# Positions in orbits of twelve: a folded transform in place of full DFT matrices, and cast loads issued by GpSimd

## The chip, the cores and the metric

The kernel runs on one core of a Trainium2 chip. The metric is the device time of one execution in microseconds. Before the change its median over three runs is 419.32 us (418.64 to 421.66). Engines are named as in the profile: PE (TensorE), DVE (VectorE), ACT (ScalarE), POOL (GpSimd), SP (SyncE).

## The reference

A linear attention with cosine and sine weights feeds a gated long convolution. The sizes are batch B = 8, heads H = 8, S = 576 positions, head dimension 64, model width 512.

```python
theta = pi/2 * arange(S) / S
phi(x) = concat([max(x, 0) * cos(theta), max(x, 0) * sin(theta)], -1)    # 64 -> 128 features
kv  = einsum('bhsf,bhsd->bhfd', phi(k), v);  z = sum(phi(k), axis=2)
x   = einsum('bhsf,bhfd->bhsd', phi(q), kv) / (einsum('bhsf,bhf->bhs', phi(q), z)[..., None] + 1e-06)
x   = x.transpose(0, 2, 1, 3).reshape(B, S, 512)
x1, x2, x3 = split(x @ w_proj, 3, axis=-1)                               # 512 columns each
conv = irfft(rfft(x2, axis=1) * rfft(filter_fft, axis=0), n=S, axis=1)   # along the positions
out  = (x1 * conv * x3) @ w_out
```

## The kernel before

All matrix work is in f16 with f32 sums. A batch's 576 positions lie in five tiles of 128 (the last holds 64; buffers are padded to 640). A framework schedules the instructions of each engine, starting from the order of the emit calls, and puts the semaphores in; pools of a fixed number of buffers say when a tile may be written again.

Batches run through a software pipeline. In cycle `cyc`, the input DMAs of batch cyc+1 are issued, the second half of the attention of batch cyc-1 is done (`emit_attn_B`), then the projections and the forward DFT of batch cyc-2 (`emit_moe_part1`), the first half of the attention of batch cyc interleaved with the transposes of batch cyc-1 (`emit_sec3`), the inverse DFT and output of batch cyc-2 (`emit_moe_part2`), and phi of batch cyc+1. In words, per batch:

- **Loads** (L203): 15 transfers by SP, one per tile of q, k and v, in f32; each position row of a head is a run of 256 B. Weights come in f32 by SP and are cast by ACT (L125) and DVE (L129, L132).
- **phi**: 20 ACT instructions (L220, L224), relu with a scale per partition, f32 to f16. DVE casts v (L228); POOL writes the column of ones (L229).
- **Attention**: PE forms kv (L264), 40 matmuls of 65 columns; transposes phi(q) (L273), 40 times 128 columns; forms the numerators (L322), 40 of 65. DVE takes reciprocals (L332, L333) and scales (L342), five instructions per head. PE transposes back per pair of heads (L291), 20 of 128; DVE (L278, L296) and ACT (L280, L298) copy transposes out of PSUM.
- **Projections**: x1 and x3 (L363, L368), 64 matmuls of 288 columns; the gate x1*x3 (L375, L376); x2 (L383), 20 of 512, evicted by ACT (L388).
- **Forward DFT** (L398, L404): 289 frequencies in tiles of 128, 128 and 33 against five position tiles, cosine and sine: 30 matmuls of 512. DVE multiplies with the filter's transform in six instructions per frequency tile (L422 to L427).
- **Inverse DFT** (L442 to L454): per channel tile of 128, cosine and sine over three frequency tiles, for 289 and for 287 positions: 48 matmuls. DVE multiplies with the gate out of PSUM (L459, L462).
- **Output** (L471), 20 of 512, ACT evicts (L476), SP stores five times (L477).

PSUM is split in three pools: 2 banks for kv, 3 for transposes, 3 for everything else. DFT tables are computed on the chip (`emit_dft_gen`, DVE and ACT); the filter is transformed in cycle 1.

## Time and profile before

| | before |
|---|---|
| median of three runs | 419.32 us |
| span of the profiled execution | 417.9 us |
| that execution's time outside the span, by the median | 1.4 us |
| PE matmul busy | 341.8 us, 82% |
| DVE busy | 237.3 us, 57% |
| ACT busy | 240.5 us, 58% |
| POOL busy | 6.6 us, 2% |
| DMA | 43.58 MB, mean 104 GB/s |

The profile is one execution. "Busy" on PE counts overlapping matmuls once, with modelled ends, so the spacing of two matmul starts says more about their cost than the duration printed. The granted TensorE clock is below full in many slices, and has to be taken with every PE figure. A batch appears in the chain of waits as a stretch of x2, DFT, inverse and output matmuls, with ACT, DVE and DMA pieces between output and the next x2.

### The profile page before, as it was taken

The page shows a single profiled execution, that of the slowest core. Times are in us where ns is not written, and L with a number is a line of the kernel's source. Part 1 is how long each engine was busy: PE and PEld are TensorE (multiplying, and loading weights), DVE is VectorE, ACT ScalarE, POOL GpSimd, SP SyncE. Part 2 cuts the span into 40 slices and gives each one's busy share as a digit, 9 for nine tenths or more (in the row PEclk, how much of TensorE's full clock was granted, in tenths as well). Part 3 has the DMA queues.
Part 4 walks back from the last instruction along what each step waited for, and adds up shares of the span by engine and source line. Part 5 has one row for each costly group of instructions (what it writes and reads, how often), then busy time and mean ns, then how long its engine had stood idle before and what let it go on. Part 6 is the DMA issues. An engine that isn't in the chain of part 4 may idle for free.

```text
span 417.9 us, 7205 instructions
## 1 busy us (share of the span) xinstructions
PE 341.8 (82%) x2606; PEld 199.5 (48%) x2606; DVE 237.3 (57%) x884; ACT 240.5 (58%) x429; POOL 6.6 (2%) x53
## 2 busy tenths in 40 slices
PE   0252937899959997699959995899979988999994
PEld 0141326546546455455546554545654546455441
DVE  5787326638394475548385739547563756372370
ACT  4993697677964677556684568358435222514502
POOL 1000000000000000000000001000000000000000
PEclk9995777699996999599999999699989997999998
DMA  9957999942677935441664064001300030003003
GB/s 183 227 208 260 227 206 170 193 91 51 164 177 119 173 89 172 107 89 25 190 143 99 0 165 127 2 13 38 115 2 0 2 113 2 0 2 113 2 0 113
DMA packets 119603, 43.58 MB, mean 104 GB/s; under 512 B 113360, under 2 KB 113360, under 8 KB 119568
## 3 DMA queue, kind: packets, MB, share of 16 engines
q1 hardware_dynamic: 119568, 43.13, 45.7%
q8 instruction: 20, 0.33, 0.3%
q14 instruction: 15, 0.12, 0.1%
HBM read 33.69 MB, written 9.44 MB: 103 GB/s over the span
## 4 chain that ended last, share of the span: by engine, by line
PE 65%; ACT 13%; DVE 10%; DMA 8%; issue 2%; SPq 1%; ACTq 0%; DVEq 0%
DVE att_pad L342 6%; DMA filt_stage<-in_moe_filter_fft_dram 2%; DMA kraw_b5t<-in_k_dram 1%; PE h_ps_f0c L183 1%; DMA vraw_b0t<-in_v_dram 1%; PE x2p_b0t L383 1%; PE x2p_b7t L383 1%; PE x2p_b6t L383 1%; PE x2p_b3t L383 1%; PE x2p_b1t L383 1%; PE out_ps_b5t L471 1%; PE x2p_b5t L383 1%; PE out_ps_b4t L471 1%; PE x2p_b4t L383 1%; PE out_ps_b3t L471 1%
## 5 line engine op out<-in xcount | busy, mean ns | idle before, releaser
L368 PEld LDWEIGHTS <-wp 128*128 128x128 f16 x256 | 27.4, 107 | 24.2 <-issue 14.6
L363 PEld LDWEIGHTS <-wp 128*128 128x128 f16 x256 | 27.7, 110 | 12.1 <-issue 1.9
L471 PEld LDWEIGHTS <-yt_pad 128*128 128x128 f16 x160 | 15.7, 98 | 17.4 <-DVE yt_pad L459 1.3
L398 PEld LDWEIGHTS <-csf 128*128 128x128 f16 (+1 forms) x120 | 10.4, 97 | 17.2 <-issue 6.8
L404 PEld LDWEIGHTS <-ssf 128*128 128x128 f16 (+1 forms) x120 | 11.7, 98 | 14.2
L291 PEld LDWEIGHTS <-att_pad 128*128 128x128 f16 x160 | 14.0, 106 | 6.4 <-DVE att_pad L342 2.5
L273 PE MATMUL qpt_ps_b0h<-identity,qp_b0t 128*128 128x128 f16 x32 | 4.4, 282 | 13.8 <-ACT qp_b0t L220 9.0
L476 ACT ACTIVATE out_sb_b7t<-out_ps_b7t 128x512 f32<-128x512 f32 (+1 forms) x5 | 3.0, 596 | 14.1 <-PE out_ps_b7t L471 11.2
L322 PE MATMUL num_ps_b0h<-kv_sb_b0g,qpt_sb_b0h 128*128 128x65 f16 x40 | 2.5, 206 | 9.5 <-DVE att_pad L342 7.8
L273 PEld LDWEIGHTS <-qp_b0t 128*128 128x128 f16 x32 | 2.8, 123 | 14.6 <-ACT qp_b0t L220 9.0
L342 DVE TENSOR_SCALAR att_pad<-num_ps_b0h,rcp_b0h 128x64 f16<-128x64 f32 (+1 forms) x40 | 8.8, 269 | 0.0
L476 ACT ACTIVATE out_sb_b6t<-out_ps_b6t 128x512 f32<-128x512 f32 (+1 forms) x5 | 3.0, 596 | 9.6 <-PE out_ps_b6t L471 8.0
L342 DVE TENSOR_SCALAR att_pad<-num_ps_b1h,rcp_b1h 128x64 f16<-128x64 f32 (+1 forms) x40 | 8.4, 268 | 0.0
L342 DVE TENSOR_SCALAR att_pad<-num_ps_b2h,rcp_b2h 128x64 f16<-128x64 f32 (+1 forms) x40 | 8.2, 268 | 0.0
L342 DVE TENSOR_SCALAR att_pad<-num_ps_b7h,rcp_b7h 128x64 f16<-128x64 f32 (+1 forms) x40 | 8.2, 269 | 0.0
L273 PEld LDWEIGHTS <-qp_pad 128*128 128x128 f16 x64 | 6.5, 108 | 3.6 <-ACT qp_pad L224 3.3
L342 DVE TENSOR_SCALAR att_pad<-num_ps_b4h,rcp_b4h 128x64 f16<-128x64 f32 (+1 forms) x40 | 8.2, 268 | 0.0
L342 DVE TENSOR_SCALAR att_pad<-num_ps_b6h,rcp_b6h 128x64 f16<-128x64 f32 (+1 forms) x40 | 8.2, 269 | 0.0
L342 DVE TENSOR_SCALAR att_pad<-num_ps_b5h,rcp_b5h 128x64 f16<-128x64 f32 (+1 forms) x40 | 8.2, 267 | 0.0
L342 DVE TENSOR_SCALAR att_pad<-num_ps_b3h,rcp_b3h 128x64 f16<-128x64 f32 (+1 forms) x40 | 8.2, 267 | 0.0
L125 ACT CAST wp<-wp_stage 128x1536 f16<-128x1536 f32 x4 | 5.9, 1474 | 3.8 <-DMA wp_stage<-in_moe_w_proj_dram 3.8
L273 PE MATMUL qpt_ps_b1h<-identity,qp_b1t 128*128 128x128 f16 x32 | 4.9, 288 | 3.5 <-ACT qp_b1t L224 2.5
(656 smaller groups left out, 1031.7 us busy)
## 6 DMA issues: line engine op xcount, KB each, us to landing
...
```

Source lines behind the costliest of these rows:

```text
L125: nc.scalar.copy(out=wp16[i], in_=wstage[("wp", i)])
L183: nc.tensor.matmul(hp[0:fs], lhs[t][0:ss, ds(ft * 128, fs)], filt16[t][0:ss], start=(t == 0), stop=(t == NST - 1),)
L273: nc.tensor.transpose(qtp[:, ds(t * 128, 128)], qp_t[(b, t)][:, h], identity)
L291: nc.tensor.transpose(xtp[:, ds(t * 128, 128)], atp[:, t], identity)
L342: nc.vector.tensor_scalar(out=atp[0:ss, t, h % 2], in0=nump[0:ss, t, 0:D], scalar1=rcp[0:ss, t : t + 1], scalar2=None, op0=AL.mult,)
L363: nc.tensor.matmul(x1p, wp16[i][:, ds(c * 128, 128)], xt_t[(b, i)][:, scol], start=(i == 0), stop=(i == NDM - 1),)
L368: nc.tensor.matmul(x3p, wp16[i][:, ds(2 * DM + c * 128, 128)], xt_t[(b, i)][:, scol], start=(i == 0), stop=(i == NDM - 1),)
L383: nc.tensor.matmul(x2p, xt_t[(b, i)][:, ds(t * 128, 128)], wp16[i][:, ds(DM, DM)], start=(i == 0), stop=(i == NDM - 1),)
L398: nc.tensor.matmul(xrp[0:fs], csf[t][:, fcol], x2t[t], start=(t == 0), stop=(t == NST - 1),)
L404: nc.tensor.matmul(xip[0:fs], ssf[t][:, fcol], x2t[t], start=(t == 0), stop=(t == NST - 1),)
L471: nc.tensor.matmul(op, yt[i][:, ds(t * 128, 128)], wo16[i], start=(i == 0), stop=(i == NDM - 1),)
L476: nc.scalar.mul(out=os_[0:ss], in_=op[0:ss], mul=OUTSC)
```

## The change

The code is rewritten around another arrangement of positions and another DFT; names of most functions change.

- **Positions**: s = 6p + j on 96 partitions, p = 0..95, j = 0..5. q and k of a batch come in one transfer each, [96, 8, 384], in which a run is six positions (1536 B in f32); v comes in six transfers straight into the buffer that has the column of ones. The GpSimd queue issues them, eight per batch, and the DMA casts f32 to f16. Three more GpSimd transfers bring the weights in f16.
- **phi** moves to DVE: 24 instructions per batch on 96 partitions x 512 (L88, called from `emit_phi`), f16 to f16.
- **Orbits**: the transposes of phi(q) multiply with a permutation (`perm`) instead of the identity; two copies (DVE L395, ACT L399) lay out 60 positions and their 60 mirror images in each tile of 128. Six positions 96 apart and their six mirror images form an orbit of twelve, on which a length-12 piece of the DFT is done at once: a matmul with the small matrix `fm` (L436, L440; 16 of 240 columns and 4 of 192) transposes the attention's result and folds it. Of its 24 groups of columns twelve feed x2 and twelve the gate.
- **DFT**: on the folded x2 it is block-diagonal, three blocks of 96x96 for cosine and sine: 6 matmuls of 512 (L480). The half-sample grid makes the inverse symmetric, so that 24 matmuls of 288 (L529) give an even and an odd part, which DVE adds and subtracts into the two halves (L534, L535), and then multiplies with the gate (L536). x2 takes 24 matmuls of 512 (L466).
- **Fewer, larger instructions** outside PE: a head pair is scaled by one DVE instruction (L421), products of the transform take two instructions of 1024 and two of 512 per block, ACT evicts up to 1024 columns at once.
- **PSUM**: one pool of four units of two banks serves all of it. The buffers for phi(q), phi(k), the attention and the output have one copy each, and raw q and k share three.
- **Loop**: `for b in range(-1, B)` with n = b + 1 in the order shown at the end of the diff. Tables for the new blocks are computed on chip (`trig`, five DVE and two ACT instructions each, 96 partitions x 288 or 864).

```diff
-    psum_kv = ctx.enter_context(tc.tile_pool(name="psum_kv", bufs=2, space=bass.MemoryType.PSUM))
-    psum_tp = ctx.enter_context(tc.tile_pool(name="psum_tp", bufs=3, space=bass.MemoryType.PSUM))
-    psum_mm = ctx.enter_context(tc.tile_pool(name="psum_mm", bufs=3, space=bass.MemoryType.PSUM))
+    psum = ctx.enter_context(tc.tile_pool(name="psum", bufs=4, space=bass.MemoryType.PSUM))
+    def unit(name):
+        return psum.tile([128, 2, 512], FP32, tag="u", bufs=4, name=name)
...
+    def emit_input_dma(b):
+        for nm, src in (("q", q), ("k", k)):
+            rw = work.tile([NP, NH, NJ * D], FP16, tag="raw", bufs=3, name=f"{nm}raw{b}")
+            raw_t[(b, nm)] = rw
+            nc.gpsimd.dma_start(out=rw, in_=src[b].rearrange("h (p j) d -> p h (j d)", j=NJ))
+        va = va_buf[b % 2]
+        vv = v[b].rearrange("h (p j) d -> p h j d", j=NJ)
+        for j in range(NJ):
+            nc.gpsimd.dma_start(out=va[:, :, j, 0:D], in_=vv[:, :, j])
+    def emit_weight_dma():
+        nc.gpsimd.dma_start(out=wp16, in_=moe_w_proj.rearrange("(i p) n -> p i n", p=128))
+        nc.gpsimd.dma_start(
+            out=filt16, in_=moe_filter_fft.rearrange("(p j) n -> p (j n)", j=NJ)
+        )
+        nc.gpsimd.dma_start(out=wo16, in_=moe_w_out.rearrange("(i p) n -> p i n", p=128))
...
+    def emit_phi(b, nm):
+        rw = raw_t[(b, nm)]
+        t = work.tile([NP, NJ, NH, 2, D], FP16, tag=f"{nm}p", bufs=1, name=f"{nm}p{b}")
+        (kp_t if nm == "k" else qp_t)[b] = t
+        for j in range(NJ):
+            for cs, col in ((0, ccol), (1, scol)):
+                tsc(
+                    t[:, j, :, cs], rw[:, :, ds(j * D, D)],
+                    col[0:NP, j : j + 1], AL.mult, 0.0, AL.max,
+                )
+    def emit_kv(b):
...
+        for h in range(NH):
+            for j in range(NJ):
+                nc.tensor.matmul(
+                    u[:, h // 4, ds((h % 4) * 65, 65)], kp[:, j, h].rearrange("p a b -> p (a b)"),
+                    va[:, h, j, 0:65], start=(j == 0), stop=(j == NJ - 1),
+                )
+        kvs = work.tile([128, 2, 4 * 65], FP16, tag="kvs", bufs=2, name=f"kvs{b}")
+        nc.scalar.copy(out=kvs, in_=u[:, :, 0 : 4 * 65])
+    def emit_qt(b, hp):
...
+        for hh in range(2):
+            for j in range(NJ):
+                nc.tensor.transpose(
+                    u[:, hh, ds(j * NP, NP)],
+                    qp[:, j, 2 * hp + hh].rearrange("p a b -> p (a b)"),
+                    perm,
+                )
+        hsl = slice(2 * hp, 2 * hp + 2)
+        nc.vector.tensor_copy(
+            out=qpt[:, hsl, :, 0, 0:60],
+            in_=u[:, :, 0:300].rearrange("p h (t c) -> p h t c", c=60),
+        )
+        nc.scalar.copy(
+            out=qpt[:, hsl, ::-1, 1, 4:64],
+            in_=u[:, :, 276:576].rearrange("p h (t c) -> p h t c", c=60),
+        )
+    def emit_num(b, hp):
...
+        for hh in range(2):
+            h = 2 * hp + hh
+            for t in range(NT):
+                nc.tensor.matmul(
+                    u[:, hh, ds(t * 65, 65)], qpt[:, h, t].rearrange("p a b -> p (a b)"),
+                    kvs[:, h // 4, ds((h % 4) * 65, 65)], start=True, stop=True,
+                )
+        nv = u[:, :, 0 : NT * 65].rearrange("p h (t e) -> p h t e", e=65)
+        rcp = work.tile([128, 2, NT], FP32, tag="rcp", bufs=2, name=f"rcp{b}_{hp}")
+        tsc(rcp, nv[:, :, :, 64], EPS, AL.add)
+        nc.vector.reciprocal(out=rcp, in_=rcp)
+        nc.vector.tensor_tensor(
+            out=att[:, :, ds(hp * 128, 128)].rearrange("p t (h d) -> p h t d", h=2),
+            in0=nv[:, :, :, 0:D],
+            in1=rcp.unsqueeze(3).to_broadcast([128, 2, NT, D]),
+            op=AL.mult,
+        )
+    def emit_fx(b):
...
+        for c in range(NC):
+            u = unit(f"fx{b}_{c}")
+            for t in range(NT - 1):
+                nc.tensor.matmul(
+                    u[:, t // 2, 0:480].rearrange("p (g o) -> p g o", o=20)[:, :, ds((t % 2) * 10, 10)],
+                    att[:, t, ds(c * 128, 128)], fm, start=True, stop=True,
+                )
+            nc.tensor.matmul(
+                cu[:, c // 2, ds((c % 2) * 256, 192)], att[:, NT - 1, ds(c * 128, 128)],
+                fm[:, :, 0:8], start=True, stop=True,
+            )
+            nc.scalar.copy(
+                out=fx[:, c, :, 0:40].rearrange("p g (u o) -> p u g o", u=2),
+                in_=u[:, :, 0:480].rearrange("p u (g o) -> p u g o", o=20),
+            )
...
+    def emit_x2(b):
...
+        for bl in range(3):
+            u = unit(f"x2_{b}_{bl}")
+            for comp in range(2):
+                for c in range(NC):
+                    nc.tensor.matmul(
+                        u[0:NP, comp],
+                        fx[:, c, ds(comp * 6 + 2 * bl, 2)].rearrange("p a b -> p (a b)"),
+                        wp16[:, c, ds(DM, DM)], start=(c == 0), stop=(c == NC - 1),
+                    )
+            nc.scalar.mul(out=x2f[:, bl], in_=u[0:NP], mul=X2SC)
+    def emit_dft(b):
...
+        for bl in range(3):
+            u = unit(f"dft{b}_{bl}")
+            for comp, tab in ((0, tre), (1, tim)):
+                nc.tensor.matmul(u[0:NP, comp], tab[:, bl], x2f[:, bl, comp], start=True, stop=True)
+            xf = work.tile([NP, 2, DM], FP16, tag="xf", bufs=2, name=f"xf{b}_{bl}")
+            nc.scalar.copy(out=xf, in_=u[0:NP])
+            m1 = work.tile([NP, 2, DM], FP16, tag="m1", bufs=1, name=f"m1_{b}_{bl}")
+            m2 = work.tile([NP, 2, DM], FP16, tag="m2", bufs=1, name=f"m2_{b}_{bl}")
+            nc.vector.tensor_tensor(out=m1, in0=xf, in1=ha[:, bl], op=AL.mult)
+            nc.vector.tensor_tensor(
+                out=m2, in0=xf, in1=hi[:, bl].unsqueeze(1).to_broadcast([NP, 2, DM]), op=AL.mult
+            )
+            nc.vector.tensor_tensor(out=yf[:, bl, 0], in0=m1[:, 0], in1=m2[:, 1], op=AL.subtract)
+            nc.vector.tensor_tensor(out=yf[:, bl, 1], in0=m1[:, 1], in1=m2[:, 0], op=AL.add)
+    def emit_gate(b, c):
...
+        for w in (0, 2):
+            u = unit(f"x{w}_{b}_{c}")
...
+            for i in range(NC):
+                for hf in range(2):
+                    nc.tensor.matmul(
+                        u[:, hf, 0:HS], wp16[:, i, ds(w * DM + c * 128, 128)],
+                        fx[:, i, ds(12 + 6 * hf, 6)].rearrange("p a b -> p (a b)"),
+                        start=(i == 0), stop=(i == NC - 1),
+                    )
+        x1s = work.tile([128, 2, HS], FP16, tag="x1s", bufs=2, name=f"x1s{b}_{c}")
+        nc.scalar.copy(out=x1s, in_=us[0][:, :, 0:HS])
+        for hf in range(2):
+            nc.vector.tensor_tensor(
+                out=(g[:, c, 0:HS] if hf == 0 else g[:, c, HS:S][:, ::-1]).rearrange(
+                    "p (j i o) -> p j i o", j=3, i=6
+                ),
+                in0=us[1][:, hf, 0:HS].rearrange("p (i j o) -> p j i o", i=6, j=3),
+                in1=x1s[:, hf].rearrange("p (i j o) -> p j i o", i=6, j=3),
+                op=AL.mult,
+            )
+    def emit_inv(b, c):
...
+        u = unit(f"inv{b}_{c}")
+        for comp, tab in ((0, ire), (1, iim)):
+            for bl in range(3):
+                nc.tensor.matmul(
+                    u[:, comp, 0:HS], yf[:, bl, comp, ds(c * 128, 128)], tab[:, bl],
+                    start=(bl == 0), stop=(bl == 2),
+                )
+        nc.scalar.copy(out=eo[:, c], in_=u[:, :, 0:HS])
+        nc.vector.tensor_tensor(out=y[:, c, 0:HS], in0=eo[:, c, 0], in1=eo[:, c, 1], op=AL.add)
+        nc.vector.tensor_tensor(out=y[:, c, HS:S][:, ::-1], in0=eo[:, c, 0], in1=eo[:, c, 1], op=AL.subtract)
+        nc.vector.tensor_tensor(out=y[:, c], in0=y[:, c], in1=g[:, c], op=AL.mult)
+    def emit_out(b):
...
+        os_ = work.tile([128, NT, DM], FP32, tag="os", bufs=1, name=f"os{b}")
+        for grp in ((0, 1), (2, 3), (4,)):
+            u = unit(f"out{b}_{grp[0]}")
+            for x, t in enumerate(grp):
+                for c in range(NC):
+                    nc.tensor.matmul(
+                        u[:, x], y[:, c, ds(OT[t], 128)], wo16[:, c],
+                        start=(c == 0), stop=(c == NC - 1),
+                    )
+            nc.scalar.mul(out=os_[:, grp[0] : grp[0] + len(grp)], in_=u[:, 0 : len(grp)], mul=OUTSC)
...
+    emit_input_dma(0)
+    emit_cols()
+    emit_weight_dma()
+    emit_pads()
+    emit_phi(0, "q")
+    emit_phi(0, "k")
+    emit_fm()
+    emit_input_dma(1)
+    emit_rows()
+    emit_fwd_tables()
+    for b in range(-1, B):
+        n = b + 1
+        if b >= 0:
+            emit_x2(b)
+        if n < B:
+            for hp in range(4):
+                emit_qt(n, hp)
+            emit_kv(n)
+        if b == 0:
+            emit_inv_tables()
+            emit_h()
+        if b >= 0:
+            emit_dft(b)
+            for c in range(NC):
+                emit_gate(b, c)
+        if n < B:
+            for hp in range(4):
+                emit_num(n, hp)
+        if n + 1 < B:
+            if n + 2 < B:
+                emit_input_dma(n + 2)
+            emit_phi(n + 1, "q")
+            emit_phi(n + 1, "k")
+        if b >= 0:
+            for c in range(NC):
+                emit_inv(b, c)
+        if n < B:
+            emit_fx(n)
+        if b >= 0:
+            emit_out(b)
```

On DVE, while the first batches start up, batch 0's attention (`rcp_b0h`, `att_pad`) stands before the change between casts of weights (`wo_`, `filt_`):

```order
L132 CAST wo_1_108<-wo_stage_242 128x512
L342 TENSOR_SCALAR att_pad_168<-num_ps_b0h_660,rcp_b0h_666 128x64 x2
L129 CAST filt_4_372<-filt_stage_238 64x512
L342 TENSOR_SCALAR att_pad_168<-num_ps_b0h_660,rcp_b0h_666 128x64
L342 TENSOR_SCALAR att_pad_168<-num_ps_b0h_660,rcp_b0h_666 64x64
L332 RECIPROCAL rcp_b0h_680<-num_ps_b0h_674 128x4
L333 RECIPROCAL rcp_b0h_680<-num_ps_b0h_674 64x1
L332 RECIPROCAL rcp_b0h_694<-num_ps_b0h_688 128x4
L342 TENSOR_SCALAR att_pad_170<-num_ps_b0h_674,rcp_b0h_680 128x64 x4
```

After the change these rows stand there; `qp_448` and `kp_461` are phi of batch 1, from its raw tiles `qraw_196` and `kraw_198`, and `att_377` is the attention of batch 0:

```order
L88 TENSOR_SCALAR qp_448<-qraw_196,ccol 96x8x64
L88 TENSOR_SCALAR qp_448<-qraw_196,scol 96x8x64
L86 TENSOR_SCALAR rcp_0_389<-num_0_378 128x10
L88 TENSOR_SCALAR kp_461<-kraw_198,ccol 96x8x64
L420 RECIPROCAL rcp_0_389<-rcp_0_389 128x10
L86 TENSOR_SCALAR rcp_1_404<-num_1_393 128x10
L421 TENSOR_TENSOR att_377<-num_0_378,rcp_0_389 128x2x5x64
L420 RECIPROCAL rcp_1_404<-rcp_1_404 128x10
L86 TENSOR_SCALAR rcp_2_419<-num_2_408 128x10
L421 TENSOR_TENSOR att_377<-num_1_393,rcp_1_404 128x2x5x64
L420 RECIPROCAL rcp_2_419<-rcp_2_419 128x10
```

Ahead of batch 0's first scaling (L421) stand now twelve rows for q of batch 1, of which the last two are shown, and one row for k of batch 1.

On DVE in the steady state, before, the end of the attention of batch 4 runs into the gate of batch 3 (`g_b3c`):

```order
L332 RECIPROCAL rcp_b4h_3021<-num_ps_b4h_3015 128x4
L342 TENSOR_SCALAR att_pad_170<-num_ps_b4h_3001,rcp_b4h_3007 128x64 x4
L342 TENSOR_SCALAR att_pad_170<-num_ps_b4h_3001,rcp_b4h_3007 64x64
L333 RECIPROCAL rcp_b4h_3021<-num_ps_b4h_3015 64x1
L342 TENSOR_SCALAR att_pad_170<-num_ps_b4h_3015,rcp_b4h_3021 128x64 x4
L342 TENSOR_SCALAR att_pad_170<-num_ps_b4h_3015,rcp_b4h_3021 64x64
L376 TENSOR_TENSOR g_b3c_3029<-x3p_b3c0h_3044,x1s_b3c0h_3053 128x288
L376 TENSOR_TENSOR g_b3c_3056<-x3p_b3c1h_3058,x1s_b3c1h_3067 128x288
L296 COPY xt_sb_b4p_3285<-xt_ps_b4p_3279 128x640
L278 COPY qpt_sb_b5h_3298<-qpt_ps_b5h_3292 128x640
```

After, the end of the attention of a batch (`att_1358`) and what follows; `kp_1442` is phi of the next batch's k:

```order
L86 TENSOR_SCALAR rcp_2_1400<-num_2_1389 128x10
L86 TENSOR_SCALAR rcp_3_1415<-num_3_1404 128x10
L420 RECIPROCAL rcp_2_1400<-rcp_2_1400 128x10
L420 RECIPROCAL rcp_3_1415<-rcp_3_1415 128x10
L421 TENSOR_TENSOR att_1358<-num_2_1389,rcp_2_1400 128x2x5x64
L421 TENSOR_TENSOR att_1358<-num_3_1404,rcp_3_1415 128x2x5x64
L88 TENSOR_SCALAR kp_1442<-kraw_946,scol 96x8x64
L88 TENSOR_SCALAR kp_1442<-kraw_946,ccol 96x8x64
```

Nine more rows of `kp_1442` follow, and then the first sum of the inverse (L534); before, no row of phi stood on DVE at all.

On POOL, before, the steady state holds memsets of the ones column, five per batch:

```order
L229 MEMSET va_pad 64x8
L229 MEMSET va_b4t_2194 128x8
L229 MEMSET va_b4t_2203 128x8
L229 MEMSET va_b4t_2212 128x8
L229 MEMSET va_b4t_2221 128x8
L229 MEMSET va_pad 64x8
```

After, it holds the input loads (`qraw`, `kraw`, `va`):

```order
L104 DMA qraw_944<-in_q_dram 96x8x384
L108 DMA va_83<-in_v_dram 96x8x64 x6
L104 DMA kraw_946<-in_k_dram 96x8x384
L104 DMA qraw_1419<-in_q_dram 96x8x384
L108 DMA va_82<-in_v_dram 96x8x64 x3
L104 DMA kraw_1421<-in_k_dram 96x8x384
```

Each of those rows is a transfer that POOL issues in this order, with the waits on its buffer in front of it.

719 lines of the change are left out of this document (296 added, 423 removed).

## The prediction

> **What bounds the kernel now.** I read the page first, then the windows from one batch's x2 to the next, then the chain of waits, and last the timelines of PE and DVE for the price of single instructions.
>
> ```profile
> span 417.9 us, 7205 instructions
> PE 341.8 (82%) x2606; PEld 199.5 (48%) x2606; DVE 237.3 (57%) x884; ACT 240.5 (58%) x429; POOL 6.6 (2%) x53
> PE 65%; ACT 13%; DVE 10%; DMA 8%; issue 2%; SPq 1%; ACTq 0%; DVEq 0%
> ```
>
> The third line is the chain by engine: 65% of the end hangs on PE. The windows, whose columns are length, busy time of PE, PEld, DVE, ACT and POOL, granted clock, DMA share and GB/s, show the start and four batches:
>
> ```profile
> 0.00:40.00 40.00, 10.04 (x120) 7.15 (x120) 27.86 (x123) 27.83 (x49) 2.26 (x23) 0.91 0.92 214
> 136.31:181.28 44.97, 39.49 (x307) 23.30 (x305) 26.73 (x100) 28.86 (x53) 1.04 (x5) 0.89 0.56 126
> 181.28:225.44 44.16, 39.39 (x324) 23.48 (x322) 27.21 (x101) 28.13 (x50) 0.56 (x5) 0.96 0.43 109
> 225.44:272.03 46.59, 41.09 (x323) 24.21 (x322) 27.20 (x101) 28.11 (x50) 1.06 (x5) 0.93 0.34 85
> 272.03:314.41 42.38, 39.48 (x324) 23.54 (x322) 25.72 (x97) 22.54 (x40) 0.00 (x0) 0.96 0.13 39
> ```
>
> A batch takes (314.41 - 136.31)/4 = 44.5 us; PE is busy for some 40 of it at a mean clock of 0.935, DVE for 27. The start is bound by DMA: 0.92 of its time is used at 214 GB/s. The chain within a batch, and the first and last output stage:
>
> ```profile
> 181.28 4.32 PE x2p_b2t L383 x20
> 185.60 1.19 PE xre_ps_b2f L398 x5
> 201.54 4.32 PE out_ps_b2t L471 x20
> 225.44 4.32 PE x2p_b3t L383 x20
> ...
> L471 PE MATMUL out_ps_b0t<-wo,yt_pad x20: 379/379/379, 108.1 to 112.2; 128*128 128x512 f16 x20
> L471 PE MATMUL out_ps_b7t<-wo,yt_pad x20: 379/379/379, 407.4 to 411.5; 128*128 128x512 f16 x20
> ```
>
> So before = 108.1 to the first output, seven steps to 407.4 (42.8 each), and 10.5 from there to the end at 417.9; 1.4 more lie outside the span (419.3 - 417.9).
>
> **The change part by part.** Prices on PE are spacings of starts. A matmul of 512 columns costs 4.32/20 = 0.216 us, by the rows above. The others:
>
> ```profile
> 207.35 0.28 PE L264 MATMUL kv_ps_b5g<-va_b5t,kp_b5t 128*128 128x65 f16 x4
> 207.47 0.20 PE L264 MATMUL kv_ps_b5g<-va_pad,kp_pad 128*128 128x65 f16 x1
> 222.34 0.65 PE L363 MATMUL x1p_b3c2h<-xt_sb_b3p,wp 128*128 128x288 f16 x4
> 222.83 0.65 PE L368 MATMUL x3p_b3c2h<-xt_sb_b3p,wp 128*128 128x288 f16 x4
> 236.28 0.39 PE L273 MATMUL qpt_ps_b5h<-identity,qp_b5t 128*128 128x128 f16 x4
> 236.50 0.22 PE L273 MATMUL qpt_ps_b5h<-identity,qp_pad 128*128 128x128 f16 x1
> 239.78 0.29 PE L446 MATMUL xc_b3c<-ssf,yim_b3f 128*128 128x289 f16 x1
> 239.90 0.29 PE L450 MATMUL xc_b3c<-crev,yre_b3f 128*128 128x287 f16 x1
> ```
>
> That is 0.03 us for 65 columns, 0.122 for 288 (gate and inverse alike), 0.055 for 128. Before, a batch is 40 kv and 40 numerators (2.4), 60 transposes (3.3), 64 gate matmuls (7.8), 20 x2 (4.3), 30 DFT (6.5), 48 inverse (5.9), 20 output (4.3): 34.5 us at full clock, 36.9 at 0.935. After: 48 kv (1.4, say 1.5) and 40 numerators (1.2), 48 transposes of 96 columns (between 0.041 and 0.055 each; 0.045 gives 2.2), 16 folds of 240 and 4 of 192 columns (0.102 and 0.081: 2.0), gate 7.8, 24 x2 (5.2), 6 DFT (1.3), 24 inverse (2.9), output 4.3: 28.4. PE loses 6.1 us per batch. That isn't the step yet, because the order after puts the stages of one batch into a ring in which DVE paces one half.
>
> DVE's prices, again from start to start:
>
> ```profile
> 212.87 0.16 DVE L332 RECIPROCAL rcp_b4h<-num_ps_b4h 128x4 f32<-128x4 f32 x1
> 212.96 0.13 DVE L333 RECIPROCAL rcp_b4h<-num_ps_b4h 64x1 f32<-64x1 f32 x1
> 222.98 0.75 DVE L228 CAST va_b6t<-vraw_b6t 128x512 f16<-128x512 f32 x2
> 235.28 0.42 DVE L425 TENSOR_TENSOR cm_b3f<-xim_sb_b3f,hre 128x512 f16<-128x512 f16 x1
> 235.62 0.42 DVE L426 TENSOR_TENSOR yre_b3f<-cm_b3f,cm_b3f 128x512 f16<-128x512 f16 x1
> 236.29 0.68 DVE L422 TENSOR_TENSOR cm_b3f<-xre_ps_b3f,hre 128x512 f16<-128x512 f32 x1
> 236.89 0.68 DVE L423 TENSOR_TENSOR cm_b3f<-xre_ps_b3f,him 128x512 f16<-128x512 f32 x1
> 239.75 0.48 DVE L278 COPY qpt_sb_b5h<-qpt_ps_b5h 128x640 f16<-128x640 f16 x1
> 240.15 0.45 DVE L459 TENSOR_TENSOR yt_pad<-xc_b3c,g_b3c 128x289 f16<-128x289 f32 x1
> 240.52 0.45 DVE L462 TENSOR_TENSOR yt_pad<-xc_b3c,g_b3c 128x287 f16<-128x287 f32 x1
> ...
> 206.53 0.60 ACT L476 ACTIVATE out_sb_b2t<-out_ps_b2t 128x512 f32<-128x512 f32 x1 [0.28 <-PE x3p_b L368]
> ```
>
> A reciprocal is 0.09, a product of 512 in f16 0.34, one that reads f32 from PSUM 0.60 (0.37 at 289), a copy of 640 0.40, an ACT eviction of 512 0.60. The two casts show 0.75 together, so the first takes about 0.75 - 0.42 = 0.33.
>
> The new phi, 24 DVE instructions of 96x512 in f16, has no row of its own. Its upper bound is the PSUM product, 0.60; below, nothing shows under half a cast, about 0.2. I take the cast, 0.33, which is one-source and works out of SBUF like phi: 4.0 us for q, 4.0 for k. [...]
>
> Now the step, in two parts by the order in which PE takes the stages. **Part A**, paced by PE: output, x2, transposes, kv, DFT, 4.3 + 5.2 + 2.2 + 1.5 + 1.3 = 14.5, at 0.93 clock 15.6. DVE's four copies (1.6) and phi of q (4.0) hide in it. Then an ACT eviction of 1024 columns, 1.2, must end before DVE can multiply. **Part B**, paced by DVE, which has to get through its queue before the last y: products 3 x (2 x 0.68 + 2 x 0.34) = 6.1; gate 8 x 0.37 = 3.0; attention, four of 640 columns at 0.75 and eight small ones at 0.09, 3.7; phi of k, 4.0, which stands in the queue between the attention and the first sum of the inverse; sums and products for y, 4 x (0.19 + 0.37 + 0.38) = 3.8, the mirrored sum priced like a PSUM read; the fold's last copy, 768 columns, 0.9. That is 21.5. PE's gate, numerators, inverse and folds, 13.9, hide beneath. The step is 15.6 + 1.2 + 21.5 = 38.3 us. ACT evicts some 20,000 columns per batch, at 0.60 per 512 23.5 us, and stays hidden. The load of a batch, 3.54 MB at 214 GB/s, is 16.5 us, and hidden. The last two steps are shorter: batch 6 without phi 34.3; batch 7 has only output, x2, DFT ((4.3 + 5.2 + 1.3)/0.93 = 11.6), 1.2 and 12.9 of DVE, 25.7.
>
> **The start.** In DVE's order batch 0's attention stands behind phi of q and one row of phi of k of batch 1, and these tiles are the 12th and 13th transfer of the GpSimd queue. Ahead of and with them come 3.54 MB of batch 0, 5.38 of weights, 2.36 of batch 1: 11.3 MB, at 214 GB/s 53 us. Then attention, the rest of phi of k, the forward tables (some 4 us) and the fold's copy bring 65. Behind stand the tables of inverse and filter, priced by
>
> ```profile
> 16.17 0.46 DVE L162 TENSOR_TENSOR gen_m<-gen_fr,gen_rr 128x289 f32<-128x289 f32 x1
> 16.54 0.31 DVE L170 TENSOR_SCALAR csf<-gen_am 128x289 f16<-128x289 f32 x1
> 16.76 0.36 DVE L154 TENSOR_SCALAR gen_fr<-srev_row,gen_col 128x287 f32<-128x287 f32 x1
> ```
>
> at 0.37 and 0.22 per 289 columns: 864 columns twice of each kind and three fills, 3.8, three times, with small pieces 13. With four copies (1.6) and 24 phi (8.0) that is 88; the filter's DFT, 42 x 0.216 = 9.1, ends at 97; DFT, eviction, and part B without phi of k (17.5) put the first output at about 118, ten later than before.
>
> The sum: 118 + 5 x 38.3 + 34.3 + 25.7 + 10.5 + 1.4 = **381 us**.
>
> **The rivals.** *POOL holds DVE* (slower). Eight transfers per batch are issued by POOL, which before did only memsets. Nothing in the trace shows what POOL pays; SP's rows for 1,024 runs are the nearest:
>
> ```profile
> 6.07 1.15 SPq L203 DMA_DIRECT2D qraw_b0t<-in_q_dram  x1
> 7.26 1.14 SPq L203 DMA_DIRECT2D kraw_b0t<-in_k_dram  x1
> ```
>
> If each transfer stops DVE's one-source instructions, or waits for them, for 1.15 us in part B, six steps with 8 x 1.15 = 9.2 us add 55, the 19 transfers of the start up to 22: 455. It decides the sign from (419 - 381)/48 = 0.8 us per transfer. For it: DVE's new phi is just the one-source kind. Against it: DVE is idle for 10 us of part A, which can swallow most. [...] Chance 0.14.
>
> *POOL is the pace* (slower). If a transfer of 768 runs costs POOL more than 38.3/8 = 4.8 us, the loads set the step. At 6 us the step is 48 (plus 58 over six steps) and the 13th transfer of the start ends at 78 instead of 53: 465. From about 5.3 us it is slower than before: 6 x (8 x 5.3 - 38.3) = 25, and 13 x 5.3 - 53 = 16. SP's 1.15 speaks against it. Chance 0.11.
>
> *Loads arrive slower*. At 150 GB/s the start is 22 longer: 403. Chance 0.10. *phi at 0.60*: five phi of k and 35 instructions of the start, 0.27 each: 16 + 9, 406. Chance 0.05.
>
> *Handovers*. PSUM now has four units, and a batch passes through some 35 of them. Each pass can cost what the trace shows between PE and ACT:
>
> ```profile
> 216.91 0.75 PE L368 MATMUL x3p_b3c0h<-xt_sb_b3p,wp 128*128 128x288 f16 x4 [1.07 <-ACT x1s_b3c0h L375]
> ```
>
> At a fifth of that, 0.2, a step grows by 7, to 45: no gain over 44.5, and 381 + 6.5 x 7 = 426 at worst; with half of it hidden 403. Chance 0.10, half of it within 1%.
>
> *Faster*: phi at 0.2 and the mirrored sums at f16 price, full clock in part A (14.5): step 34.8, 355 to 365. Chance 0.12.
>
> **How the numbers follow.** My case, 365 to 400, has 0.38. A measurement of this kernel tells 1% (4 us) from no change. Faster: 0.38 + 0.12 + 0.10 + 0.05 and 0.02 of the handovers, 0.67; within 1%: 0.05; slower: both POOL rivals and the rest of the handovers, 0.28. The range from 345 to 440 takes in everything but the outer part of the POOL rivals and a still faster phi.
>
> **What would show it.** Right: the profile after has steps near 38 us between outputs; DVE at about 27 us per step with no gap from the first product to the last y; PE idle before the output for DVE; the first output near 118, batch 0's attention waiting for k of batch 1. Wrong: phi rows above 0.5 or stretched unevenly (POOL holds DVE); POOL busy all through and PE or DVE waiting for `qraw` or `kraw` in the steady state (POOL is the pace); PE waiting for ACT in most units (handovers); a first output far from 118.

## The result: 330.6 us, 21% less

The changed kernel takes 330.59 us (median of four, 329.89 to 330.73) against 419.18: a ratio of 0.788, with a 95% interval of 0.784 to 0.792. The forecast was 381, with a range from 345 to 440: the sign was right, the size was not, and the time lies below the range. The page of the changed kernel, span, engines and chain by engine:

```profile
span 328.9 us, 6111 instructions
PE 268.2 (82%) x2394; PEld 181.5 (55%) x2394; DVE 226.7 (69%) x702; ACT 170.4 (52%) x228; POOL 55.2 (17%) x80
PE 56%; DVE 25%; DMA 8%; ACT 6%; issue 2%; POOL 1%; ACTq 0%; DVEq 0%; POOLq 0%
```

DVE's part of the chain has gone from 10% to 25%; PE's busy share is 82% as before, in less time. The windows, by the same columns as before, from one batch's x2 to the next:

```profile
131.79:165.09 33.30, 29.93 (x295) 20.72 (x292) 25.05 (x73) 19.74 (x26) 6.13 (x8) 1.00 0.60 78
165.09:198.59 33.50, 30.12 (x294) 20.88 (x294) 25.36 (x74) 19.74 (x26) 6.13 (x8) 1.00 0.69 90
198.59:232.05 33.46, 30.08 (x295) 20.89 (x295) 25.32 (x74) 19.74 (x26) 5.43 (x7) 1.00 0.61 83
232.05:266.17 34.12, 31.54 (x295) 22.04 (x296) 24.97 (x74) 19.75 (x26) 0.00 (x0) 0.95 0.12 36
```

Three of these steps take 33.4 us and the last 34.1, where the windows before had 44.5 on average and 38.3 was forecast, and PE is granted its full clock in three of the four. The chain of waits shows the first and the last output, and between them one step in pieces:

```profile
94.31 3.83 PE out L548 x17
...
172.85 2.04 PE qt L389 x48
174.89 1.53 PE kv L376 x48
176.42 1.31 PE dft L480 x6
177.72 7.96 PE x L503 x64
185.83 0.41 DVE yf L489
186.24 0.34 DVE yf L490
186.58 1.46 DVE g L511 x4
188.44 0.84 DVE att L421 x2
...
190.48 1.46 DVE att L421 x2
191.94 2.88 DVE kp L88 x11
195.47 0.37 DVE y L536
...
317.43 4.21 PE out L548 x18
```

In this chain PE paces the step up to the end of the gate (L503) and DVE from there to the last y. The prediction had the change of hands one stage earlier, at DVE's first product, and DVE's rows have no gap from that product (179.16) to the last y (198.9) either, so DVE is full beside PE's gate. By the two outputs, 417.9 - 328.9 = 89 us come as 14 from the start (first output at 94.3 instead of 108.1), 76 from the seven steps (223.1 instead of 299.3; a mean of 31.9 instead of 42.8, as the last steps are shorter), and one is given back at the end (11.5 instead of 10.5).

### The profile page after: what moved, and what is told of

The parts are those of the page before. It is cut to its first block, busy times and chain, and to the rows that moved or that the text cites. A ratio compares the mean times of both kernels' runs of the same rounds, so it can differ in the third digit from the quotient of the medians.

```text
span 328.9 us, 6111 instructions
## 1 busy us (share of the span) xinstructions
PE 268.2 (82%) x2394; PEld 181.5 (55%) x2394; DVE 226.7 (69%) x702; ACT 170.4 (52%) x228; POOL 55.2 (17%) x80
## 3 DMA queue, kind: packets, MB, share of 16 engines
q0 software_dynamic: 51344, 16.85, 47.4%
q1 hardware_dynamic: 5760, 9.44, 10.1%
HBM read 33.69 MB, written 9.44 MB: 131 GB/s over the span
## 4 chain that ended last, share of the span: by engine, by line
PE 56%; DVE 25%; DMA 8%; ACT 6%; issue 2%; POOL 1%; ACTq 0%; DVEq 0%; POOLq 0%
PE x L503 14%; PE x L466 14%; PE out L548 8%; DMA qraw<-in_q_dram 6%; PE inv L529 5%; PE qt L389 4%; DVE att L421 4%; PE h_ps L342 4%; DVE g L511 3%; DVE kp L88 3%; ACT fx L444 3%; DMA kraw<-in_k_dram 2%; PE kv L376 2%; PE dft L480 2%; DVE qp L88 2%
## 5 line engine op out<-in xcount | busy, mean ns | idle before, releaser
L503 PE MATMUL x<-fx,wp 128*128 128x288 f16 x512 | 64.4, 286 | 0.0
L503 PEld LDWEIGHTS <-wp 128*128 128x128 f16 x512 | 50.0, 98 | 14.4 <-issue 0.2
L395 DVE COPY qpt<-qt 128x600 f16<-128x600 f16 x32 | 14.9, 468 | 56.7 <-PE qt L389 56.0
L108 POOL DMA_DIRECT2D va<-in_v_dram x48 | 37.3, 782 | 97.6 <-PE kv L376 88.8
L466 PE MATMUL x<-wp,fx 128*96 128x512 f16 x192 | 46.4, 397 | 3.9 <-DVE fx L448 3.9
L548 PE MATMUL out<-wo,y 128*128 128x512 f16 x160 | 38.4, 379 | 7.2 <-DVE y L536 3.6
L466 PEld LDWEIGHTS <-fx 128*96 128x96 f16 x192 | 24.3, 129 | 24.7 <-DVE fx L448 5.8
L533 ACT CAST eo<-inv 128x576 f16<-128x576 f32 x32 | 20.4, 638 | 33.5 <-PE inv L529 32.2
L444 ACT CAST fx<-fx 128x960 f16<-128x960 f32 x32 | 28.7, 980 | 14.2 <-PE fx L436 14.2
L471 ACT ACTIVATE x2f<-x 96x1024 f16<-96x1024 f32 x24 | 24.4, 1018 | 19.8 <-PE x L466 19.8
L389 PE MATMUL qt<-perm,qp 96*128 96x96 f16 x384 | 20.5, 215 | 12.1 <-DVE qp L88 11.5
L436 PE MATMUL fx<-fm,att 128*128 128x240 f16 x128 | 19.2, 286 | 11.3 <-DVE att L421 9.1
L529 PEld LDWEIGHTS <-yf 96*128 96x128 f16 x192 | 19.7, 107 | 13.7 <-DVE att L421 5.8
L511 DVE TENSOR_TENSOR g<-x,x1s 128x288 f16<-128x288 f32 x64 | 26.6, 445 | 0.0
L482 ACT CAST xf<-dft 96x1024 f16<-96x1024 f32 x24 | 23.4, 1013 | 4.7 <-DVE m L486 4.7
L88 DVE TENSOR_SCALAR qp<-qraw,ccol 96x512 f16<-96x512 f16 x48 | 19.3, 403 | 8.3 <-DMA qraw<-in_q_dram 8.3
L421 DVE TENSOR_TENSOR att<-num,rcp 128x640 f16<-128x640 f32 x32 | 25.0, 817 | 0.0
```

Source lines behind the costliest of these rows:

```text
L88: nc.vector.tensor_scalar(out=out, in0=in0, scalar1=s1, scalar2=s2, op0=op0, op1=op1)
L108: nc.gpsimd.dma_start(out=va[:, :, j, 0:D], in_=vv[:, :, j])
L389: nc.tensor.transpose(u[:, hh, ds(j * NP, NP)], qp[:, j, 2 * hp + hh].rearrange("p a b -> p (a b)"), perm,)
L421: nc.vector.tensor_tensor(out=att[:, :, ds(hp * 128, 128)].rearrange("p t (h d) -> p h t d", h=2), in0=nv[:, :, :, 0:D], in1=rcp.unsqueeze ...
L444: nc.scalar.copy(out=fx[:, c, :, 0:40].rearrange("p g (u o) -> p u g o", u=2), in_=u[:, :, 0:480].rearrange("p u (g o) -> p u g o", o=20),)
L466: nc.tensor.matmul(u[0:NP, comp], fx[:, c, ds(comp * 6 + 2 * bl, 2)].rearrange("p a b -> p (a b)"), wp16[:, c, ds(DM, DM)], start=(c == 0) ...
```

## The experiments

Times are medians; the ratio in brackets is to the kernel before, with its 95% interval. The changed kernel's own is 330.6 (0.784 to 0.792).

**Transfers on POOL, their number and run length.** Every q and k in six transfers of 256 B runs:

```diff
-            nc.gpsimd.dma_start(out=rw, in_=src[b].rearrange("h (p j) d -> p h (j d)", j=NJ))
+            sv = src[b].rearrange("h (p j) d -> p h j d", j=NJ)
+            for j in range(NJ):
+                nc.gpsimd.dma_start(out=rw[:, :, ds(j * D, D)], in_=sv[:, :, j])
```

> The changed kernel, with q and k of a batch loaded by six cast transfers each, as v is, so that every run in HBM is 256 B instead of 1536 B, and POOL issues 18 transfers per batch instead of 8. If the early start of the changed kernel comes from long runs, the tile of q of batch 1 lands near 45 us instead of 30.3 and the first output moves from 94 to about 108; if it comes from the cast (half the bytes written), it stays near 30. On POOL as the pace: 18 transfers at the 0.77 us seen are 14 us per step of 33.4, so the step should not move but for stops of DVE. On POOL holding DVE: the changed kernel shows about 0.24 us of delay to one phi instruction per transfer that meets phi; ten more transfers per batch would add up to 2.4 us per step (17 in all) if all of them met DVE work on the path, and nothing if they fall into DVE's idle time. Forecast 345 with long runs as the cause, 331 to 340 with the cast.

343.3 us (0.815 to 0.825). The steps stay at 33.5 (outputs in the chain at 180.39, 213.90 and 247.41): in the steady state neither pace nor stop of POOL counts at 18 transfers per batch. The first output comes at 109.0 instead of 94.3, but not for the reason given: q of batch 1 is complete at 36.3, six us later than in the changed kernel, and not at 45. Those six us fit POOL's time for issuing: it is busy with the 18 transfers of batch 0 until 15.1, and the weights are issued at 15.4 instead of 7.8. The larger part of the loss stands in the same queue further on:

```profile
57.72 0.50 POOL L300 IOTA sr_i<- 96x288 int32 x1
76.52 4.07 PE L344 MATMUL h_ps<-filt,hc 96*96 96x512 f16 x9 [17.82 <-DVE tn_h L88]
```

POOL writes the row of indices for the inverse's tables (`sr_i`) behind the 18 transfers of batch 2, at 57.7 where the changed kernel has it at 39.8. DVE makes the tables after that, and the filter's first matmul starts at 76.5 instead of 61.2, which covers all of the loss. The run changes the length of the runs and the number of transfers together, and it is the number that shows; what short runs cost is read from the kernel before, below.

**No loads in the steady state** (phi of batches 2 to 7 reads batch 1's tiles, and v stays that of batches 0 and 1):

```diff
     def emit_input_dma(b):
+        if b >= 2:
+            for nm in ("q", "k"):
+                raw_t[(b, nm)] = raw_t[(1, nm)]
+            return
```

> The changed kernel without the input transfers of batches 2 to 7; phi of these batches reads the tiles of batch 1, and v stays. Left out: those loads. If POOL's transfers hold DVE or pace the step, the steps shrink: three stretched phi instructions per step, 0.24 us each, end on DVE's way to the first product of the transform, so 0.7 us per step and 4 us in all at most. If the loads are hidden, the time stays within 1 us of 330.6. A step shorter by over 2 us would mean that the loads cost more than the stretched rows show.

323.6 us (0.770 to 0.778), 7 less, more than forecast. A step is 32.8 us, 0.6 shorter, which is the forecast; in the profiled execution, with 319.3 us the fastest of five, the first output also comes 5.2 us earlier (89.1). There the matmuls of the filter take 6.04 instead of 8.01 us, at a granted clock that was 0.66 in that stretch of the changed kernel (61 to 76 us) and is 1.00 here. Whether the loads or something else lowered it isn't separated. In the changed kernel's timeline of DVE the stops are seen directly, as gaps between starts of phi, and POOL's row shows what it did then:

```profile
176.36 0.35 DVE L88 TENSOR_SCALAR qp<-qraw,ccol 96x512 f16<-96x512 f16 x1
176.62 0.35 DVE L88 TENSOR_SCALAR qp<-qraw,scol 96x512 f16<-96x512 f16 x1
176.88 0.54 DVE L88 TENSOR_SCALAR qp<-qraw,ccol 96x512 f16<-96x512 f16 x1
177.35 0.33 DVE L88 TENSOR_SCALAR qp<-qraw,scol 96x512 f16<-96x512 f16 x1
177.61 0.61 DVE L88 TENSOR_SCALAR qp<-qraw,ccol 96x512 f16<-96x512 f16 x1
178.14 0.33 DVE L88 TENSOR_SCALAR qp<-qraw,scol 96x512 f16<-96x512 f16 x1
178.40 0.58 DVE L88 TENSOR_SCALAR qp<-qraw,ccol 96x512 f16<-96x512 f16 x1
178.90 0.33 DVE L88 TENSOR_SCALAR qp<-qraw,scol 96x512 f16<-96x512 f16 x1
...
176.55 2.31 POOL L108 DMA_DIRECT2D va<-in_v_dram  x3 [14.17 <-PE kv L376]
```

Phi starts every 0.26 us; behind three of its rows, while POOL issues three transfers, the next start comes after 0.47 to 0.53. The size is 0.2 to 0.3 us for each of the three, not 1.15.

**Transposes, kv and both phi ahead of x2**, so that DVE has phi to do while PE is at x2:

```diff
-        if b >= 0:
-            emit_x2(b)
         if n < B:
             for hp in range(4):
                 emit_qt(n, hp)
             emit_kv(n)
+        if b >= 0 and n + 1 < B:
+            if n + 2 < B:
+                emit_input_dma(n + 2)
+            emit_phi(n + 1, "q")
+            emit_phi(n + 1, "k")
+        if b >= 0:
+            emit_x2(b)
...
-        if n + 1 < B:
+        if b < 0:
```

> The changed kernel with another order in the loop: transposes and kv of batch n come before x2 of batch b, and both phi of the next batch are emitted right behind them. In the changed kernel DVE sits idle for 8 us from the last y to the first transpose copy, since phi of q waits for the transposes to read the single buffer, and then phi of k (2.9 us) stands between the attention and y. My theory is that DVE's queue from the first product to the last y paces 20 us of the step of 33.4, and phi of q the entry to it. Then this order takes 2.9 + 1.4 us off a step: 29 to 30 us, 6 steps, 330.6 - 25 = 305. The rival is that PE already paces the step (28.4 us of matmuls at full clock, 82% busy): then the step can't fall under 31 to 32 and the time is 318 to 325.

324.4 us (0.768 to 0.778). The step is 31.15 us (x2 at 140.95, 172.10, 203.25), as the rival had it: with phi out of DVE's second half PE, busy for 29.6 of 31.15 us, is the limit. The steps give 14 us, and eight at the start (first output at 102.4 instead of 94.3) take back more than half. kv of batch 1 doesn't wait for v there: it starts on PE at 47.3, right behind the transposes. What waits is DVE:

```profile
59.52 0.31 DVE L300 CAST srow<-sr_i 96x288 f32<-96x288 int32 x1 [5.38 <-POOL sr_i L298]
```

The indices for the inverse's tables stand in POOL's queue again, this time behind the transfers of batch 3, which the new order issues ahead of them: 59.1 instead of 39.8. The filter's first matmul starts at 69.8 instead of 61.2.

**q and k of batch 1 ahead of the weights** in POOL's queue (`emit_input_dma(1)` without v before `emit_weight_dma()`, v of batch 1 after it):

> The changed kernel with the transfers of q and k of batch 1 ahead of the weights in POOL's queue. Batch 0's attention stands behind phi of q of batch 1 on DVE, and in the changed kernel that q lands at 30.3 us, behind 5.4 MB of weights. If this order sets the start, attention begins near 22 instead of 34 us and the first output moves from 94 by 5 to 10 us earlier, 321 to 326 in all; if the weights, which then land later, or the tables on DVE set the start, the time stays within 2 us of 330.6.

322.9 us (0.765 to 0.774). The first output comes at 86.3 instead of 94.3, the attention's first row on DVE at 23.4 instead of 33.7. So eight us of the start hang on batch 0's attention standing behind batch 1's q, as the prediction read it from DVE's order.

**Both orders, batch 0 as in the changed kernel:**

> The changed kernel with both orders: q and k of batch 1 ahead of the weights, and from batch 1 on transposes, kv and both phi ahead of x2. The second had a step of 31.15 instead of 33.4 but a start some 8 us later, since it put kv of batch 1, and so a wait for v, ahead of x2 of batch 0; here batch 0 keeps the old order. If the two gains add, 322.9 - 5 x 2.3 = 311, between 308 and 314.

308.9 us (0.732 to 0.736), as forecast: the gains add, and with the old order for batch 0 the eight us at the start are not lost. Steps of 31.15 from batch 1 on, first output at 86.5. This beats both kernels, by 21.7 us under the changed one.

**More matmuls in either half.** Each DFT matmul four times, or each group of inverse matmuls twice:

```diff
-                nc.tensor.matmul(u[0:NP, comp], tab[:, bl], x2f[:, bl, comp], start=True, stop=True)
+                for rep in range(4):
+                    nc.tensor.matmul(u[0:NP, comp], tab[:, bl], x2f[:, bl, comp], start=True, stop=True)
```

> The changed kernel with each of the six DFT matmuls done four times over: 18 more matmuls of 512 columns at 0.216 us, 3.9 us of PE per batch, ahead of the gate matmuls. If PE paces this part of a step (through DFT and gate up to the attention), the step grows by 3 to 3.9 and the time to 354 to 362. If DVE alone paces everything from the first product on, PE catches up and the time stays under 340.

> The changed kernel with each group of three inverse matmuls done twice: 24 more matmuls of 288 columns at 0.122 us, 2.9 us of PE per batch, while DVE still has 11 phi of k ahead of y. My theory is that DVE paces this part, so the step grows by 0.5 to 1.5 at most (the folds come later) and the time is 334 to 343. If PE paces the whole step, as its 82% busy share suggests, it is 331 + 8 x 2.9 = 354.

346.3 us (0.817 to 0.825) and 341.0 us (0.805 to 0.813). Of 3.9 us per step 1.8 come through in the first (x2 at 172.03 and 207.26, 35.2 apart), less than forecast; of 2.9 some 1.2 in the second (34.6), as forecast. Added work on PE counts by less than half in both halves, so PE alone doesn't pace either of them; the step is a ring of both engines.

**The kernel before, with fewer DFT matmuls.** Forward only the last position tile, inverse only one of the two products per half:

```diff
-            for t in range(NST):
-                nc.tensor.matmul(
-                    xrp[0:fs], csf[t][:, fcol], x2t[t],
-                    start=(t == 0), stop=(t == NST - 1),
-                )
+            nc.tensor.matmul(xrp[0:fs], csf[NST - 1][:, fcol], x2t[NST - 1], start=True, stop=True)
...
```

> The kernel before, with as many DFT matmuls as the changed one: only the last position tile enters the forward DFT (6 matmuls instead of 30), and half of the inverse is left out (24 instead of 48); 8.1 us of PE per batch go. Left out: that part of both sums. If PE paced the old step, it falls from 42.8 to 35 and the time to 354 to 362, and most of the gain of the change comes from the matmuls alone. If ACT's phi and the attention on DVE take over, the step falls to 38 to 40 only, 385 to 400, and the rest of the gain belongs to phi and the larger instructions.

420.2 us (0.996 to 1.002): no gain, outside both forecasts. The window of one step of this run:

```profile
224.81:269.47 44.66, 37.36 (x275) 21.86 (x274) 27.49 (x101) 27.39 (x50) 0.56 (x5) 0.81 0.33 85
```

48 matmuls fewer per step than before, yet PE is busy 37 us and the step is no shorter than the 44.5 of before: the granted clock is 0.81 where the same step had 0.93. From x2 to the end of the output, the first row before and the second in this run:

```profile
225.44:250.00 24.56, 24.56 (x149) 12.25 (x148) 12.22 (x30) 15.11 (x25) 0.00 (x0) 1.00 0.40 98
224.81:250.50 25.69, 23.34 (x137) 11.18 (x135) 12.89 (x31) 14.96 (x26) 0.00 (x0) 0.80 0.36 91
```

The stretch that lost the matmuls is as long as before. The old kernel has no gap on PE there, at full clock: its DFT matmuls cover DVE's products. Without them PE waits, 2.3 us in all, for the products and for ACT, and the clock is 0.80.

**phi on DVE in the kernel before**, alone and with the fewer matmuls:

```diff
-                nc.scalar.activation(
-                    out=dst[0:ss, :, 0], in_=rw[0:ss],
-                    func=AF.Relu, scale=cos_col[0:ss, t : t + 1],
-                )
...
+                for f, col in ((0, cos_col), (1, sin_col)):
+                    nc.vector.tensor_scalar(
+                        out=dst[0:ss, :, f], in0=rw[0:ss], scalar1=col[0:ss, t : t + 1],
+                        scalar2=0.0, op0=AL.mult, op1=AL.max,
+                    )
```

> The kernel before with phi on DVE (one multiply-and-maximum per half, f32 to f16) instead of ACT: 20 instructions of about 0.6 us leave ACT per batch, 20 of about 0.33 come to DVE. Taking 8 us of matmuls from PE had changed nothing, so something else sets the step. If it is phi in ACT's queue, between the evictions that PE waits for, the step falls from 42.8 towards the 36.9 that PE needs, 375 to 395 in all. If it is the chain through DVE's attention, or the order as such, the time stays at 412 to 425.

> The kernel before with phi on DVE and with only 6 forward and 24 inverse DFT matmuls (the rest of both sums left out). If phi on ACT had hidden the gain of the smaller DFT, it appears now: 8 us per step under the run with phi on DVE alone, 330 to 350. If PE is not the next limit, the two runs with phi on DVE lie within 10 us of each other.

422.8 us (0.997 to 1.028) and 425.4 us (1.008 to 1.035). ACT loses 12 us per batch and the step doesn't notice. In the second, the chain shows where PE stands, and what the matmuls behind it cost:

```profile
193.38 0.68 DVE cm_b2f L411
194.06 0.60 DVE cm_b2f L412
194.66 0.60 DVE cm_b2f L413
195.26 0.61 DVE cm_b2f L414
...
204.14 6.23 PE out_ps_b2t L452 x20
```

The inverse waits for products on DVE, and the output's twenty matmuls, 4.32 us in the kernel before, take 6.23. From 130 to 310 us this run has a granted clock of 0.83, where a step of the kernel before had 0.93 (225.44 to 272.03). Whether PE's waits between stages lower it, and which of them, these rows don't show.

**Cast loads by POOL in the kernel before** (raw tiles in f16, `nc.gpsimd.dma_start`, runs of 256 B as they were):

> The kernel before with its 15 loads per batch issued by POOL, cast to f16 on the way, in the same runs of 256 B; the weights stay with SP in f32. If the cast alone speeds the start, DMA moves batch 0 and 1 with half the bytes written and the first output comes at about 100 instead of 108, 410 in all; the steps should not move if POOL's transfers neither hold DVE nor pace anything. If the short runs limit the rate in f32 and f16 alike, the time stays at 419. If 15 transfers of 1,024 runs cost POOL over 2.8 us each, the step grows past 42.8.

449.2 us (1.064 to 1.088), slower; a longer step had been forecast only for transfers of over 2.8 us. A transfer costs POOL 0.87 us, so 15 of them don't pace a step of 48. But they stand in one queue, each behind the wait of the one ahead, and the memsets too:

```profile
169.65 0.88 POOL L203 DMA_DIRECT2D qraw_b4t<-in_q_dram  x1 [13.06 <-ACT qp_b4t L224]
...
183.50 0.40 POOL L229 MEMSET va_b5t<- 128x8 f16 x4 [5.64 <-PE kv_ps_b4g L264]
185.04 0.87 POOL L203 DMA_DIRECT2D kraw_b5t<-in_k_dram  x1 [1.06 <-ACT kp_b5t L224]
```

The first output comes at 124.6 and the steps are 48 us. How much is this queue and how much the transfers themselves isn't separated. Cast loads in this order and with these runs are no gain.

**The place of the gate, in both directions.** In the kernel before, the block of L350 to L377 moves behind the DFT loop; in the changed kernel, `emit_gate` moves ahead of `emit_x2`:

> The kernel before with the gate's 64 matmuls moved from ahead of x2 to behind the forward DFT, as the changed kernel has them; nothing else differs. Neither fewer DFT matmuls nor phi on DVE had moved the old step of 42.8 us; its chain shows PE standing between the DFT and the inverse for the evictions and products, and at the cycle's start for the attention on DVE. If that order sets the step, 7.8 us of gate matmuls now cover the products and the step falls to 37 to 39, 380 to 395 in all. If only the sum of all cuts counts, it stays at 412 to 425.

> The same order in the kernel before, with 6 forward and 24 inverse DFT matmuls (the rest of both sums left out). If the order is what kept the smaller DFT from paying, this run is 5 to 8 us per step under the run with the order alone, 335 to 360. If the attention on DVE or the granted clock takes the gain again, the two lie within 15 us of each other.

> The changed kernel with the gate's matmuls ahead of x2, where the old kernel had them. If the place of the gate is a cause of the shorter step, PE now stands behind the DFT until DVE's products are done, 4 to 6 us per step, and the time is 362 to 378. If DVE's queue as a whole sets the step, the time stays under 345, since DVE's work is the same.

The old kernel with the late gate: 414.8 us (0.985 to 0.993), 1%. That is far from the 380 to 395 of the theory and inside the rival's 412 to 425: the order alone isn't the cause, since the old kernel has no gap on PE behind the DFT for the gate to fill (24.56 of 24.56 us busy, above). With fewer matmuls as well: 383.3 us (0.894 to 0.920). The same cut that was worth nothing under the old order is worth 31 us under the new one, less than forecast. The changed kernel with the early gate: 372.9 us (0.882 to 0.897), 42 worse, as forecast. Its chain behind the DFT:

```profile
272.12 3.14 DVE qp L88 x12
275.26 0.60 DVE m L485
...
281.56 0.34 DVE yf L489
281.95 5.42 PE inv L529 x22
```

From the transposes' end at 271.6 to 281.95 PE is busy for 5.1 us (kv, DFT, numerators) and waits for the other 5.2, for phi, products and attention; that is the 4 to 6 us per step that were forecast. Its inverse then costs 5.42/22 = 0.246 us per matmul, twice the 0.122 of the old rows, in a step with a mean granted clock of 0.91 (254.17 to 293.20). That these waits lowered the clock isn't shown: the changed kernel has its inverse at both prices. The first step's and a later one's:

```profile
119.70:125.70 6.00, 5.96 (x26) 3.77 (x27) 5.97 (x21) 1.91 (x3) 0.12 (x1) 0.50 0.01 3
189.20:192.40 3.20, 3.12 (x25) 2.29 (x26) 3.17 (x11) 1.83 (x3) 0.00 (x0) 1.00 0.00 0
```

The inverse waits 0.70 us for the attention in both, and the four groups of numerators ahead of it wait 0.2 to 0.3 us each in both.

**The attention's instructions, in both directions.** In the changed kernel ten of 64 columns per pair of heads instead of one of 640 (the old form of L342); in the old kernel with late gate and fewer matmuls two per head instead of five:

> The changed kernel with its attention scaled as before, by ten DVE instructions of 64 columns per pair of heads instead of one of 640. At 0.19 us each, from the old rows, a pair takes 1.9 instead of 0.75 us, 4.6 more per step. The attention stands in DVE's queue ahead of phi of k and y, so I expect all of it in the step: 330.6 + 8 x 4.6 = 367, between 358 and 370. If PE or the folds hide it, under 345.

> The kernel before with three things of the changed one: the gate late, 6 forward and 24 inverse DFT matmuls (the rest of both sums left out), and the attention scaled by two DVE instructions per head instead of five. Undoing the last in the changed kernel cost 32 us. If these three make the step, the time falls from 383 by 20 to 30, to 353 to 363, with a step near 37; what is left to 330.6 is then the start (14 us) and phi and evictions. If the attention's instructions matter only in the changed kernel's order, it stays over 372.

362.6 us (0.860 to 0.870): 32 worse, as forecast, with a step of 39.0. Its chain runs through forty of them:

```profile
199.04 2.03 DVE att L423 x11
201.12 1.81 DVE att L423 x9
...
203.45 3.83 DVE att L423 x20
207.29 2.88 DVE kp L88 x11
```

And 360.7 us (0.851 to 0.861) in the old kernel, 23 less, as forecast. So three parts together, the gate behind the DFT, the smaller DFT and the larger attention instructions, take the old kernel from 420 to 361, two thirds of the whole gain, with loads, phi and positions as they were. The gate and the attention instructions were also taken back in the changed kernel, where each costs more than 30 us.

## Why the prediction was wrong

- **The order of the step was right.** PE paces a first half, DVE the second, and phi of k stands between attention and y on the path (2.88 us in the chain). The sum of DVE's half, 21.5, came to 19.7 (first product at 179.16 to the last y at 198.9, without a gap). Two of its terms were too dear: phi, priced by a cast from f32 at 0.33, costs 0.26 from start to start; the mirrored sums, priced like a PSUM read at 0.37, cost 0.22 like the others. No row of the kernel before shows the 0.2 at which the case "faster" had phi; what the changed kernel shows is 0.26.
- **Part A was mis-sized most in the step.** 15.6 and the eviction's 1.2, 16.8 in all, became 13.8. Nine of the twenty output matmuls (1.9 us) run before the last y, since three of the four channel tiles of y are ready by then; the sum had put all twenty behind it. And the clock, taken as 0.93 from the old windows, is 1.00 in most new ones: 1.1 us. The case "faster" had the clock, with a chance of 0.12, but not the output. The stage is not PE's alone: DVE stands idle for 8 us in it, and phi of q then holds the first product back (its input is evicted near 178, the product starts at 179.16).
- **The start was mis-sized by 24 us**: first output at 94.3 instead of 118. The step that failed is "at 214 GB/s 53 us", with 19 of the 24 (the attention's first row stands at 33.7): the 214 was a mean over 40 us in which the old kernel loaded at three rates, and it was used as the rate of other runs in another order. The windows of the kernel before, inputs in runs of 256 B, then weights in runs of 2 to 6 KB, then a stretch almost without loads:

```profile
3.00:16.00 13.00, 2.38 (x15) 1.10 (x15) 6.99 (x36) 8.65 (x17) 0.00 (x0) 1.00 1.34 222
20.00:24.00 4.00, 1.19 (x8) 0.87 (x9) 3.44 (x12) 4.00 (x10) 0.00 (x0) 1.00 1.00 400
25.00:29.00 4.00, 2.87 (x58) 2.63 (x55) 2.61 (x12) 4.00 (x7) 0.41 (x5) 1.00 0.08 17
```

  The last column is GB/s. What DVE waits for in the changed kernel:

```profile
30.27 0.35 DVE L88 TENSOR_SCALAR qp<-qraw,ccol 96x512 f16<-96x512 f16 x1 [8.35 <-DMA qraw<-in_q_dram]
```

  By 30.3 us 10.1 MB of f32 have been read (3.54 + 5.38 + 1.18), since 1.3 us: 350 GB/s, and k lands before 33.8. (The page counts the f16 bytes that are written, 16.85 MB on this queue for 33.69 read, so its GB/s are half of that.) f32 in runs of 2 to 6 KB went at 400 without a cast, so the length of the runs may be enough to explain the rate; that the cast adds to it isn't shown. That batch 0's attention waits for batch 1's q was right, and the run with the other order shows what it is worth, 8 us.
- **Steps and start together** are 251.5 - 223.1 = 28 and 24 us, the 50 by which the forecast was high but for one at the end and rounding. All these errors point one way, and the range, built from rivals that mostly pointed the other way, had no case in which rate, clock and overlap are all better.
- **The POOL rivals**, 0.25 of the chance, fell: 0.77 us per transfer, 0.2 to 0.3 us of stop in each of three rows of phi per step, 33.5 us per step with 18 transfers. At the start POOL's queue does count, as two of the runs show (15 and 8 us), by what stands behind the transfers in it. **Handovers** fell as well: PE's waits for ACT are short rows of 0.2 to 0.5 us, 2.6 in four steps, and PE is busy for 30 of 33.4.
- "65% of the end hangs on PE" was a true row and said little about the old kernel: with 8 us of matmuls per batch gone nothing was faster. The prediction didn't build on it, but it doesn't explain the old step either. The runs do: with the gate early the DFT matmuls cover DVE's products, and taking them out only opens waits there; with the gate late the smaller DFT pays. The waits that the old PE does have lie at the cycle's start (6.8 us busy from 205.9 to 217.0), 1.8 us for the attention on DVE and the rest for ACT's evictions, and with the late gate and the smaller DFT the larger attention instructions gain 23 us.
- Two sums of the prediction are off by little: the terms of the first POOL rival, 381 + 55 + 22, give 458 and not 455, and a set of tables at the prices shown is 4.2 us and not 3.8. Nothing hangs on either.

What stays open: whether the cast adds anything to the loading rate; what lowers the clock to 0.66 during the filter's DFT and to 0.50 in the first step's inverse; and which of loads, phi, evictions and positions makes the last 30 us from 361 to 331.
